# Local and summary attention with a spatially gated MLP: transposes, mixing and plan changed

## Chip, cores and metric

The kernel runs on one core of one Trainium2 chip, as one launch. The metric is the device time of that core in microseconds. The core has five engines that work side by side, each through its own instructions in a fixed order: TensorE (PE, matmuls and transposes; PEld is its loading of weights), VectorE (DVE), ScalarE (ACT), GpSimd (POOL) and SyncE (SP), from whose queue nearly all DMAs are issued.

## The reference

Attention, for batch 4, 8 heads, sequence 768, head size 64, in float32: every query looks at the keys nearer than 16 positions, and beside them at 24 summaries, one for each block of 32 positions. A summary key is the maximum over its block, a summary value the mean.

```
k_sum = k.reshape(B, H, nb, 32, D).max(axis=3)
v_sum = v.reshape(B, H, nb, 32, D).mean(axis=3)
scores_l = where(|i - j| < 16, q @ k.T / 8, -1e9)
scores_s = q @ k_sum.T / 8 + log(32)
a = softmax(concat([scores_l, scores_s], -1))       # eps 1e-9 in the denominator
x = (a @ concat([v, v_sum])), heads side by side     # 4 x 768 x 512
h = relu(x @ w_in);  u, v = halves of h              # 512 each
v_n = (v - mean) / sqrt(var + 1e-6)
out = (u * (w_spatial @ v_n + b_spatial)) @ w_out    # 4 x 768 x 512
```

`w_in` (512 x 1024) and `w_out` (512 x 512) arrive as float64, all else as float32.

## The kernel before

**Attention** goes in 24 groups: 4 batches, 3 chunks of 256 positions (`c`), 2 sets of 4 heads (`g`). For one group, `scores` (L411) makes 16 products of 64 queries with 120 keys (64 + 2 x 16 near ones and 24 summaries), in half-array tiles, into PSUM tile `s`. Each of the two "heads" `a` of a group (in fact two heads stacked on the 128 partitions) then has its softmax in four pieces on DVE (L425) and ScalarE (L429), the inverse of the sums (L434, L435) and a scaling (L437). `trans` (L450) turns the probabilities over on TensorE, 8 transposes of 64 rows for each head, into one PSUM tile `t` of two banks of 512 float32 that both heads share; two copies bring it to SBUF (`pt`), one by ScalarE and one by DVE, after both heads. `mix` (L468) multiplies by the values `ve` (16 products of 64 columns), and the result is split into two `fp32r` parts, high and low, on ScalarE (`xh`, L481) and DVE (`xl`, L482).

Scores, transposes and mixing of a group use half of the array's rows, columns or both at a time, while the dense tiles use the full array; so do the transposes of value means, `vmp` (L381), with all 128 partitions, 128 moving columns and 88 weight columns.

**The dense part** of a batch has four kinds of tiles: `proj_v` (6 tiles `pv`, 12 matmuls of 512 columns each), `proj_u` (`pu`: 4 tiles of 12 x 512 and 4 of 12 x 256), `spatial` (`sp`: 4 of 18 x 512 and 4 of 18 x 256) and `proj_out` (`po`, 6 of 12 x 512). `mm3` (L501) makes each product of high and low parts as three matmuls, hence steps of three that an attention piece can come between. The four share three one-bank PSUM tiles `m`.

**Weights** come by DMA and are split into high and low parts on ScalarE, DVE and POOL: `w_in` for `v` first (`wwi` matmuls help), then for `u`, `w_spatial` (`ws`) and `w_out` (`wo`).

**The order** of all engines is written out ahead by a planner, `Plan`. Each step is added with the engines that can do it and a duration for each, a priority, and what it reads and writes. `order` then always takes the step that can start first, the lower priority among equals, and places it on the engine that ends it first. A step's result counts as there after `LAG` of its engine, for TensorE's use a further `SLACK` of 500 ns later. A DMA's arrival is modelled by `WIRE` and a rate, and at most eight are under way. The order that comes out is fixed: an engine whose next instruction waits runs nothing else. Priorities are times in microseconds: attention group `i` has `at(i)`, and the dense tiles follow a counter `dense`. Where the plan leaves TensorE idle before a point early in the kernel, throw-away matmuls (`warm`, L670) fill the time.

```python
    SLOTS = dict(s=1, t=1, x=1, m=3, k=4, vt=1, p=4, pt=3, ...
    LAG = dict(PE=250, ACT=150, DVE=150, POOL=150, SP=0)
                t = min(from_(op, at, e) for e in op.engs)
                if best is None or (t, op.pri, op.n) < best:
                u.ready = max(u.ready, op.end if e == "PE" and "PE" in u.engs else done + (SLACK if "PE" in u.engs else 0))
```

Of the kernel before, what the change touches and what calls it, by code (L numbers as in the profile page):

```python
# [59 lines left out]
class Op:  # L60
    __slots__ = ("engs", "fn", "pri", "after", "users", "need", "ready", "bufs", "start", "end", "eng", "n", "port", "xfer")


class Plan:


    SLOTS = dict(s=1, t=1, x=1, m=3, k=4, vt=1, p=4, pt=3, x01h=2, x01l=2, x2h=2, x2l=2, g=NG, e=3, u=1, vnh=1, vnl=1,
# [3 lines left out]
    LAG = dict(PE=250, ACT=150, DVE=150, POOL=150, SP=0)  # L71

    def __init__(self):
        self.ops, self.wrote, self.read, self.turn, self.late = [], {}, {}, {}, set()

    def add(self, engs, fn, pri, w=(), r=(), port=False, xfer=0):
# [4 lines left out]
        op.fn, op.pri, op.users, op.n = fn, pri, [], len(self.ops)  # L81
        op.port, op.xfer = port, xfer
# [13 lines left out]
        for x in (*w, *r):  # L96
            if isinstance(x, Buf) and not x.ops and x.tag in self.TURNS and x.args[4][:2] not in self.OUT_OF_TURN :
# [7 lines left out]
    def order(self):  # L105
# [4 lines left out]
        waiting = {}  # L110
# [7 lines left out]
        made, landed, wire, port = [], [], 0, 0  # L118
# [9 lines left out]
        while pool:  # L128
# [20 lines left out]
            op.end = op.start + op.engs[e]  # L149
            op.eng = e  # L150
# [9 lines left out]
            done = op.end + self.LAG[e]  # L160
# [19 lines left out]
def tile_local_summary_attention_gmlp(ctx: ExitStack, tc: tile.TileContext, qT, kext, vpad, vnat, vT, w_in, w_sp, b_rep, w_out, maskc, out):  # L180
# [39 lines left out]
    def early(name):  # L220
        return EARLY.get(name, 0.0)

    def dma(out_, in_, kb, pri, w=(), r=(), issue=420, rate=RATE):
        add(("SP", issue), lambda e: nc.sync.dma_start(out=out_() if callable(out_) else out_, in_=in_() if callable(in_) else in_), pri, w, r, xfer=kb * 1024 / rate)
# [12 lines left out]
    def split32(src, hi, lo, name, pri, key):  # L237

        n = src.shape[-1]
        st = Buf(moe, [P, 2 * TH], F32, "g", name)  # L240
        dma(lambda: st.t[:, :n], src, n * 0.5, pri + early("d" + key[1:]), w=[st])
        pri += early(key)
        add(("ACT", act_ns(n)), lambda e: nc.scalar.copy(out=hi, in_=st.t[:, :n]), pri, w=[key + "h"], r=[st])
        add(two_ns(n), lambda e: eng(e).tensor_sub(out=lo, in0=st.t[:, :n], in1=hi), pri, w=[key + "l"], r=[st, key + "h"], port=True)

    def split64(st, so, f, fo, src, hi, lo, pri, key, on_pe=False):

        if src.dtype != I64:
            n = src.shape[-1]
            dma(lambda: st.t[:, so:so + n], src, n * 0.5, pri, w=[(st, so), st])  # L250
            add(("ACT", act_ns(n)), lambda e: nc.scalar.copy(out=hi, in_=st.t[:, so:so + n]), pri, w=[key + "h"], r=[(st, so), st])
            add(two_ns(n), lambda e: eng(e).tensor_sub(out=lo, in0=st.t[:, so:so + n], in1=hi), pri, w=[key + "l"], r=[(st, so), st, key + "h"], port=True)
            return
# [6 lines left out]
        dma(raw, src.bitcast(I32), n, pri + early("d" + key[1:]), w=[kr], r=[st])  # L260
        pri += early(key)

        add(("ACT", act_ns(n)), lambda e: nc.scalar.activation(out=fv(), in_=words(1).bitcast(F32), func=AF.Copy, scale=2.0 ** -112), pri, w=[kf], r=[kr, st, f])
        add(("DVE", n * 0.72 + 60), lambda e: nc.vector.tensor_scalar(out=fi(), in0=fi(), scalar1=3, scalar2=None, op0=ALU.logical_shift_left), pri, w=[kf], r=[st, f], port=True)
        add(("DVE", n * 1.05 + 65), lambda e: nc.vector.scalar_tensor_tensor(
            out=fi(), in0=words(1), scalar=-2 ** 31, in1=fi(), op0=ALU.bitwise_and, op1=ALU.bitwise_or), pri, w=[kf], r=[kr, st, f], port=True)

        add(("DVE", n * 0.72 + 60), lambda e: nc.vector.tensor_scalar(out=words(1), in0=fi(), scalar1=-2 ** 23, scalar2=None, op0=ALU.bitwise_and), pri, w=[kr + (1,)], r=[kr, kf, st, f], port=True)
        add(("ACT", act_ns(n)), lambda e: nc.scalar.copy(out=hi, in_=fv()), pri, w=[key + "h"], r=[kf, f])
        add(("DVE", n * 1.05 + 65), lambda e: nc.vector.scalar_tensor_tensor(  # L270
            out=words(0).bitcast(F32), in0=words(0).bitcast(U32), scalar=2.0 ** -52, in1=words(1).bitcast(F32),
            op0=ALU.mult, op1=ALU.mult), pri, w=[kr + (0,)], r=[kr, kr + (1,), st, f], port=True)
        if on_pe:
# [7 lines left out]
            add(("PE", 2000), mm, pri, w=[ps], r=[key + "h", kf, kr + (0,), st, f, negid[0]])  # L281
            add(dict(ACT=act_ns(n), DVE=dve_ns(n)), lambda e: copy(e, lo, ps.t[:, :n]), pri, w=[key + "l"], r=[ps])
# [6 lines left out]
    def win_load(half, pri):  # L289
# [5 lines left out]
        for c in range(NC):  # L295
            if half == 0 and c > 1:
                for o in range(0, DF, TH):
                    st = Buf(moe, [P, 2 * TH], F32, "g", f"wi{half}_{c}_{o}")
                    f = Buf(moe, [P, DF], F32, "e", f"wf{half}_{c}_{o}")
                    first(st, f, pri)  # L300
# [3 lines left out]
            if c % 2 == 0:  # L304
                tag = ("u", None, "vnl", "vnh")[2 * half + c // 2]
                stages[c // 2] = Buf(big, [P, 3 * 1024], F32, tag, f"wi{half}_{c}")
                first(stages[c // 2], None, pri)
# [24 lines left out]
    def key_load(b, pr, pri):  # L332
        kt = k_sb[b, pr] = Buf(att, [P, KC], F32, "k", f"k{b}_{pr}")
        dma(lambda: kt.t, kext[b, pr], 544, pri, w=[kt])

    def key_prep(b, pr, pri):
        kt = k_sb[b, pr]
        gm = Buf(small, [P, 52], F32, "gm", f"gm{b}_{pr}")

        def emit(e):  # L340
# [32 lines left out]
    def vmean(b, pr, pri, buf):  # L373
        vt = Buf(att, [P, S], F32, "vt", f"vt{b}_{pr}")
        dma(lambda: vt.t, vT[b, pr], 384, pri + VT_OFF, w=[vt])
        vs = vs_in[:, pr * SEG:(pr + 1) * SEG]
        add(("DVE", 880), lambda e: nc.vector.tensor_reduce(
# [3 lines left out]
        add(("PE", 110), lambda e: nc.tensor.transpose(out=ps.t[:SEG, :P], in_=vs, identity=ident), pri, w=[ps, f"ves{buf}_{pr % 2}"], r=[f"vs{pr}"])  # L381
# [5 lines left out]
    def q_load(b, c, g, buf, pri):  # L387
        dma(qd[buf], qT[b, c, g], 256, pri, w=[f"q{buf}"])

    def v_load(b, c, g, buf, pri):  # L390
        s0 = c * CH
        fs = slice(2 * g * P, 2 * (g + 1) * P)
        dma(ve[buf][:QB], vpad[b, s0:s0 + CH, fs].rearrange("(i p) f -> p i f", p=QB), 256, pri, w=[f"vea{buf}"], issue=620, rate=RATE_64)
        dma(ve[buf][SEG:],
            vpad[b, s0 + QB:s0 + QB + CH, fs].rearrange("(i p) f -> p i f", p=QB)[:2 * WIN], 128, pri, w=[f"veb{buf}"], issue=620, rate=RATE_32)
# [3 lines left out]
    def scores(b, c, pg, buf, pri):  # L399


        ps = Buf(ps_s, [P, 2, 512], F32, "s", f"s{b}_{c}_{pg}")
        kts = [k_sb[b, 2 * pg + r] for r in range(2)]
# [10 lines left out]
        add(("PE", 1000), mm, pri, w=[ps], r=[*kts, f"q{buf}"])  # L414
# [3 lines left out]
    def softmax(u, ps, pri):  # L418
        b, c, pg, a = u
        pt = p_sb[u] = Buf(att, [P, BPU, KW], F32, "p", f"p{b}_{c}_{pg}_{a}")  # L420
        st = Buf(sums, None, None, "st", f"st{b}_{c}_{pg}_{a}")
        for i in range(BPU):
            g = c * BPU + i
            mi = 0 if g == 0 else (2 if g == NSEG - 1 else 1)
            add(("DVE", 205), lambda e, i=i, mi=mi: nc.vector.tensor_tensor_reduce(  # L425
# [5 lines left out]
                accum_out=st.t[:, 1, i:i + 1]), pri, w=[(pt, i)], r=[pt, st])  # L431

        def inverse(e):
            nc.vector.tensor_scalar_add(out=st.t[:, 1, :], in0=st.t[:, 1, :], scalar1=EPS_SM)  # L434
            nc.vector.reciprocal(out=st.t[:, 0, :BPU], in_=st.t[:, 1, :BPU])  # L435
        add(("DVE", 380), inverse, pri, w=[(pt, "i")], r=[(pt, i) for i in range(BPU)] + [st, pt])
        add(dict(DVE=590, POOL=1080), lambda e: eng(e).tensor_tensor(  # L437
# [3 lines left out]
    def trans(b, c, pg, pri):  # L441


        ps = Buf(ps_t, [P, 2, 512], F32, "t", f"t{b}_{c}_{pg}")
        for a in range(2):
            def mm(e, a=a, pt=p_sb[b, c, pg, a]):
                for i in range(BPU):
                    for r in range(2):
                        hs = slice(r * QB, (r + 1) * QB)
                        nc.tensor.transpose(out=ps.t[:KW, r, a * CH + i * QB:a * CH + (i + 1) * QB], in_=pt.t[hs, i, :], identity=ident[hs, hs])  # L450
            pt = p_sb.pop((b, c, pg, a))
            add(("PE", 300), mm, pri, w=[(ps, a)], r=[(pt, "n"), pt, ps])
        for r in range(2):
            tt = pt_sb[b, c, 2 * pg + r] = Buf(att, [KW, 2 * CH], F32, "pt", f"pt{b}_{c}_{pg}_{r}")
            add(dict(ACT=510, DVE=600), lambda e, tt=tt, r=r: copy(e, tt.t, ps.t[:KW, r]), pri, w=[tt], r=[(ps, 0), (ps, 1), ps])
# [3 lines left out]
    def mix(b, c, g, buf, pri):  # L459
        ps = Buf(ps_x, [P, 2, CH], F32, "x", f"x{b}_{c}_{g}")  # L460
        tts = [pt_sb.pop((b, c, 2 * g + r)) for r in range(2)]

        def mm(e):
            for r in range(2):
                for n in range(BPU):
                    for a in range(2):
# [4 lines left out]
                            rhs=tts[r].t[:, a * CH + n * QB:a * CH + (n + 1) * QB],  # L471
                            start=True, stop=True)
        add(("PE", 1050), mm, pri, w=[ps], r=[*tts, f"vea{buf}", f"veb{buf}", f"ves{buf}_0", f"ves{buf}_1"])
# [7 lines left out]
        add(("ACT", 520), lambda e: nc.scalar.copy(out=h.t[:, :, fs], in_=ps.t), pri, w=[kh], r=[ps, h])  # L481
        add(("DVE", 610), lambda e: nc.vector.tensor_sub(out=l.t[:, :, fs], in0=ps.t, in1=h.t[:, :, fs]), pri, w=[kl], r=[ps, kh, h, l])  # L482
# [35 lines left out]
    def proj_v(b, t, pri):  # L518
        s = batch_state(b)
        c, o = divmod(t * P, CH)  # L520
        ps = Buf(ps_m, [P, 512], F32, "m", f"pv{b}_{t}")
# [237 lines left out]
```

## Time and profile before

| | |
|---|---|
| median of 3 runs | 427.93 us (427.31 to 428.41) |
| span of the profiled execution | 426.5 us, 9422 instructions |
| between the two | 1.4 us |
| PE busy | 413.7 us (97%), 3604 matmul records |
| DVE / ACT / POOL busy | 269.2 (63%) / 214.1 (50%) / 52.8 (12%) |
| HBM | 40.16 MB read, 6.29 MB written |

The page gives no time of the profiled execution other than its span, from the first instruction to the last; the difference to the median is what lies around it. Records of matmuls overlap, since matmuls are pipelined: the record of a 512-column matmul in the dense part is some 390 ns long, while the next starts some 227 ns later. So the distances between starts, and the chain of waits, which cuts pieces where the next begins, are the way to price TensorE's work. The granted clock (PEclk) is a share of full speed, which is 2.4 GHz; a half is 1.2 GHz. In the chain of waits, `x6` behind a piece counts its instructions. A scores or mixing matmul in float32 is recorded as two instructions, so `s x32` is 16 products.

### The profile page before, as it was taken

How to read it: one execution, taken by the hardware profiler on the slowest of the kernel's cores; microseconds unless marked ns; L12 is line 12 of the kernel's file. 1: busy time of each engine (PE TensorE's matmuls, PEld its weight loads, DVE VectorE, ACT ScalarE, POOL GpSimd, SP SyncE). 2: the span in 40 equal slices, each digit the busy share in tenths (PEclk: the TensorE clock that was granted, in tenths of full speed). 3: DMA queues.
4: the chain of work that ended last, by engine and by line, in shares of the span. 5: the costliest groups of instructions: out<-in, count | busy, mean ns of one | idle time of the engine just before them, and what ended most of it. 6: DMA issues, size and time to landing. Idle time of an engine off the chain costs nothing.

```text
span 426.5 us, 9422 instructions
## 1 busy us (share of the span) xinstructions
PE 413.7 (97%) x3604; PEld 333.0 (78%) x3604; DVE 269.2 (63%) x927; ACT 214.1 (50%) x655; POOL 52.8 (12%) x72
## 2 busy tenths in 40 slices
PE   8999977999999999999999999999999999999995
PEld 8557755788887878788787877788787978898884
DVE  4778999889993988384661967366582546135402
ACT  5389965686263656463442657364273344231221
POOL 1046843110000012010000001110000002010000
PEclk9999996999999999999999999999999999999998
DMA  7998999151025942322023652102103010000021
GB/s 291 382 319 234 269 274 270 34 162 38 0 63 164 330 132 68 99 77 60 4 63 112 209 165 62 38 26 62 38 26 112 26 51 1 0 2 0 2 98 49
DMA packets 25741, 47.06 MB, mean 110 GB/s; under 512 B 2528, under 2 KB 12640, under 8 KB 25568
## 3 DMA queue, kind: packets, MB, share of 16 engines
q1 hardware_dynamic: 25616, 46.33, 35.6%
q8 instruction: 28, 0.46, 0.4%
q10 hardware_dynamic: 80, 0.13, 0.1%
q14 instruction: 17, 0.14, 0.1%
HBM read 40.16 MB, written 6.29 MB: 109 GB/s over the span
## 4 chain that ended last, share of the span: by engine, by line
PE 90%; DMA 7%; ACT 1%; DVE 1%; POOL 0%; issue 0%; DVEq 0%; SPq 0%; POOLq 0%
PE sp L501 24%; PE pu L501 16%; PE po L501 16%; PE pv L501 14%; PE x L468 5%; PE s L411 5%; DMA ve<-in_vpad_dram 4%; PE t L450 3%; PE warm L670 3%; DMA ws<-in_w_sp_dram 2%; PE vsum L364 1%; PE wwi L280 1%; PE wwi L278 1%; PE vmp L381 0%; DVE p L425 0%; ACT ve L383 0%
## 5 line engine op out<-in xcount | busy, mean ns | idle before, releaser
L429 ACT ACTIVATE p<-p,sums 128x120 f32<-128x120 f32 x192 | 73.5, 385 | 4.6 <-DVE sums L425 4.5
L501 PE MATMUL sp<-wsp_h,vnh 128*128 128x512 f32 (+1 forms) x192 | 66.6, 347 | 0.0
L501 PE MATMUL sp<-wsp_l,vnh 128*128 128x512 f32 (+1 forms) x192 | 64.7, 337 | 0.0
L501 PE MATMUL sp<-wsp_h,vnl 128*128 128x512 f32 (+1 forms) x192 | 64.5, 336 | 0.0
L425 DVE CUSTOM_DVE_ANT_0 p<-s,mask 128x120 f32<-128x120 f32 x192 | 42.1, 277 | 17.9 <-PE s L411 17.7
L501 PE MATMUL po<-wo_h,gt 128*128 128x512 f32 x128 | 48.1, 404 | 0.0
L501 PE MATMUL pu<-xh,win_h 128*128 128x512 f32 (+1 forms) x128 | 44.7, 349 | 0.0
L573 ACT CAST gt<-g 128x512 fp32r<-128x512 f32 (+1 forms) x32 | 16.4, 512 | 55.2 <-DVE g L566 52.0
L501 PE MATMUL pu<-xl,win_h 128*128 128x512 f32 (+1 forms) x128 | 43.2, 337 | 0.0
L501 PE MATMUL pu<-xh,win_l 128*128 128x512 f32 (+1 forms) x128 | 43.0, 336 | 0.0
L501 PE MATMUL pv<-win_h,xh 128*128 128x512 f32 x96 | 41.0, 427 | 1.6 <-ACT ve L383 1.6
L501 PEld LDWEIGHTS sp<-wsp_h,vnh 128*128 128x128 f32 x192 | 36.3, 189 | 5.5 <-issue 1.1
L501 PEld LDWEIGHTS sp<-wsp_h,vnl 128*128 128x128 f32 x192 | 36.4, 190 | 4.0
L501 PEld LDWEIGHTS sp<-wsp_l,vnh 128*128 128x128 f32 x192 | 36.4, 190 | 3.5
L501 PE MATMUL pv<-win_l,xh 128*128 128x512 f32 x96 | 38.3, 399 | 0.0
L565 DVE TENSOR_TENSOR g<-sp,brep 128x512 f32<-128x512 f32 (+1 forms) x32 | 17.6, 552 | 32.7 <-PE sp L501 32.7
L501 PE MATMUL pv<-win_h,xl 128*128 128x512 f32 x96 | 38.0, 396 | 0.0
L501 PE MATMUL po<-wo_l,gt 128*128 128x512 f32 x96 | 37.6, 392 | 0.0
L429 ACT ACTIVATION_READ_ACCUMULATOR p<-p,sums 128x1 f32 x192 | 36.3, 189 | 0.0
L535 POOL TENSOR_TENSOR mv<-mv,mhalf 128x1 f32<-128x1 f32 x24 | 16.6, 694 | 135.4 <-DVE mv L533 127.8
L482 DVE TENSOR_TENSOR xl<-x,xh 128x512 fp32r<-128x512 f32 x24 | 16.5, 688 | 22.4 <-ACT xh L481 22.3
L595 ACT COPY ob<-po 128x512 f32<-128x512 f32 x23 | 13.5, 587 | 33.8 <-PE po L501 28.2
(106 smaller groups left out, 786.7 us busy)
## 6 DMA issues: line engine op xcount, KB each, us to landing
k<-in_kext_dram SPq DMA_DIRECT2D x16, 544.0 KB, 7.5
qd<-in_qT_dram SPq DMA_DIRECT2D x24, 256.0 KB, 4.5
ve<-in_vpad_dram SPq DMA_DIRECT2D x24, 256.0 KB, 3.8
out_dram<-ob SPq DMA_DIRECT2D x23, 256.0 KB, 2.0
vt<-in_vT_dram SPq DMA_DIRECT2D x12, 384.0 KB, 3.6
wi<-in_w_in_dram SPq DMA_DIRECT2D x6, 512.0 KB, 5.5
ve<-in_vpad_dram SPq DMA_DIRECT2D x24, 128.0 KB, 3.6
wo<-in_w_out_dram SPq DMA_DIRECT2D x8, 256.0 KB, 6.6
```

What stands on the lines that cost most here:

```text
L411: nc.tensor.matmul(out=ps.t[r * QB:(r + 1) * QB, a, i * KW:(i + 1) * KW], lhsT=qt[hs, r, i], rhs=kts[r].t[hs, g * SEG:g * SEG + KW], start ...
L425: add(("DVE", 205), lambda e, i=i, mi=mi: nc.vector.tensor_tensor_reduce(out=pt.t[:, i, :], in0=ps.t[:, a, i * KW:(i + 1) * KW], in1=mask[ ...
L429: add(("ACT", 380), lambda e, i=i: nc.scalar.activation(out=pt.t[:, i, :], in_=pt.t[:, i, :], func=AF.Exp, scale=-1.0, bias=st.t[:, 0, i:i ...
L450: nc.tensor.transpose(out=ps.t[:KW, r, a * CH + i * QB:a * CH + (i + 1) * QB], in_=pt.t[hs, i, :], identity=ident[hs, hs])
L468: nc.tensor.matmul(out=ps.t[a * D:(a + 1) * D, r, n * QB:(n + 1) * QB], lhsT=ve[buf][:, n, o:o + D], rhs=tts[r].t[:, a * CH + n * QB:a * C ...
L482: add(("DVE", 610), lambda e: nc.vector.tensor_sub(out=l.t[:, :, fs], in0=ps.t, in1=h.t[:, :, fs]), pri, w=[kl], r=[ps, kh, h, l])
L501: nc.tensor.matmul(out=ps.t[:, :n], lhsT=x, rhs=y, start=(j == i == 0), stop=(j == last and i == 2))
L535: add(("POOL", 500), lambda e: nc.gpsimd.tensor_tensor(out=mv.t[:, 1:2], in0=mv.t[:, 1:2], in1=mhalf, op=ALU.pow), pri, w=[mv])
L565: add(("DVE", dve_ns(n)), lambda e: nc.vector.tensor_add(out=g.t[:, :n], in0=ps.t[:, :n], in1=brep[:, ts]), pri, w=[g], r=[ps, "brep"])
L573: add(("ACT", act_ns(n)), lambda e: nc.scalar.copy(out=gh[1](), in_=g.t[:, :n]), pri, w=[kh], r=[g, gt])
L595: add(("ACT", 520), lambda e: nc.scalar.copy(out=ob.t, in_=ps.t), pri, w=[ob], r=[ps])
L670: nc.tensor.matmul(out=warm.t[:, :KW], lhsT=ident, rhs=ident[:, :KW], start=True, stop=True)
```

## The change

- **Transposes.** A head's 8 transposes of 64 rows become 4 of 128 rows, into a one-bank tile `t` of its own. There is one slot for such a tile, so the second head's transposes follow the first head's copy. A copy now belongs to a head, and mixing reads the new layout.
- **PSUM.** The bank that comes free makes a fourth projection tile `m`.
- **Mixing and scores.** From group 8 on, scores of a group and mixing of the group before are one step of the plan: the 32 instructions of the mixing, directly behind them the 32 of the scores. That makes 16 such pairs. The first group of the next batch is added ahead of the dense tiles of a batch.
- **Planner.** Durations and lags are other figures; a change of tile mode on TensorE is charged (187 ns to or from full-array mode, 143 between the two others); several DVE steps are split into their single instructions; `SLACK` falls from 500 to 2, and `RATE` rises from 330 to 365. A two-engine step that is planned to start before 46 us goes to POOL unless DVE would end it 56 us sooner.
- **Offsets.** A table `SHIFT` of 151 entries adds to the priority of single steps; `d...` are DMAs (`dws`, `dwo`: spatial and output weights).

The diff, cut to its core:

```diff
-    SLOTS = dict(s=1, t=1, x=1, m=3, ...
-    LAG = dict(PE=250, ACT=150, DVE=150, POOL=150, SP=0)
+    SLOTS = dict(s=1, t=1, x=1, m=4, ...
+    LAG = dict(PE=240, ACT=140, DVE=120, POOL=90, SP=0)
+    TURN_ROUND, TURN_OVER = 187, 143
...
+        op.fn, op.pri, op.users, op.n = fn, pri + SHIFT.get(op.tag, 0.0), [], len(self.ops)
...
+            if e == "PE":
+                if op.mode[0] != mode:
+                    op.end += self.TURN_ROUND if "d" in (op.mode[0], mode) else self.TURN_OVER
+                mode = op.mode[-1]
...
-        add(("PE", 1000), mm, pri, w=[ps], r=[*kts, f"q{buf}"])
+        if with_ is None:
+            add(("PE", S_NS), mm, pri, w=[ps], r=[*kts, f"q{buf}"], mode="s")
+        else:
+            mix_, pri_, wm, rm, after = with_
+
+            def both(e):
+                mix_(e)
+                mm(e)
+            plan.tag = f"xs{b}_{c}_{pg}"
+            add(("PE", X_NS + S_NS + Plan.TURN_OVER), both, pri_, w=[*wm, ps], r=[*rm, *kts, f"q{buf}"], mode="xs")
+            after()
...
-        ps = Buf(ps_t, [P, 2, 512], F32, "t", f"t{b}_{c}_{pg}")
         for a in range(2):
-            def mm(e, a=a, pt=p_sb[b, c, pg, a]):
+            ps = Buf(ps_t, [P, 512], F32, "t", f"t{b}_{c}_{pg}_{a}")
+            pt = p_sb.pop((b, c, pg, a))
...
+            def mm(e, a=a, pt=pt, ps=ps):
                 for i in range(BPU):
-                    for r in range(2):
-                        hs = slice(r * QB, (r + 1) * QB)
-                        nc.tensor.transpose(out=ps.t[:KW, r, a * CH + i * QB:a * CH + (i + 1) * QB], in_=pt.t[hs, i, :], identity=ident[hs, hs])
...
-            add(("PE", 300), mm, pri, w=[(ps, a)], r=[(pt, "n"), pt, ps])
...
+                    nc.tensor.transpose(out=ps.t[:KW, i * P:(i + 1) * P], in_=pt.t[:, i, :], identity=ident)
+            add(("PE", 340), mm, pri, w=[ps], r=[(pt, "n"), pt])
+            tt = pt_sb[b, c, pg, a] = Buf(att, [KW, 2 * CH], F32, "pt", f"pt{b}_{c}_{pg}_{a}")
+            add(dict(ACT=psa_ns(512), DVE=dve_ns(512)), lambda e, tt=tt, ps=ps: copy(e, tt.t, ps.t[:KW]), pri, w=[tt], r=[ps])
...
-                            rhs=tts[r].t[:, a * CH + n * QB:a * CH + (n + 1) * QB],
+                            rhs=tts[a].t[:, n * P + r * QB:n * P + (r + 1) * QB],
...
-        mix(b, c, g, buf, pri + early(f"x{i}"))
+        m = mix(b, c, g, buf, pri)
+        if i + 1 >= MERGE_FROM and i + 1 < NGRP:
+            waiting.append((m[0], at(i + 1) - LEAD, *m[2:]))
+        else:
+            plan.tag = f"xs{b}_{c}_{g}x"
+            add(("PE", X_NS), m[0], m[1], w=m[2], r=m[3], mode="x")
+            m[4]()
...
-        for i in range(2 * NCH * b, 2 * NCH * (b + 1)):
+        for i in range(2 * NCH * b + (b > 0), min(2 * NCH * (b + 1) + 1, NGRP)):
...
+U_BIG, MERGE_FROM, LEAD = 2, 8, 0.0
+SHIFT = dict(
...
+    dv0_0_0=3, dv0_0_1=106, dv0_1_0=257, dv1_1_0=36, dv2_0_0=263, dvn=38, dvt1_0=469, dvt1_1=13, dwi0_2_256=108,
...
+    dwo1_256=467, dwo2_0=599, dwo2_256=628, dwo3_0=418, dwo3_256=45, dws0_0=575, dws0_512=491, dws1_0=8, dws1_512=518,
...
-SLACK = 500.0
-FAVOUR, BUSY = 1760.0, 55780.0
-WIRE, RATE, RATE_64, RATE_32 = 2200, 330.0, 210.0, 195.0
+SLACK = 2.0
+FAVOUR, BUSY = 56326.0, 46130.0
+WIRE, RATE, RATE_64, RATE_32 = 2300, 365.0, 188.0, 208.0
+S_NS, X_NS = 816, 916
...
+def psa_ns(n):
+    return 58 + n * 0.828
```

## Rows read from the trace of the kernel before

**Rows 1.** Windows: per stretch busy us (x instructions) of PE, PEld, DVE, ACT, POOL; PEclk, DMA, GB/s

```profile
2.50:39.40 36.90, 36.20 (x366) 26.38 (x365) 26.63 (x105) 24.80 (x78) 9.12 (x11) 1.00 0.95 331
39.40:61.60 22.20, 22.15 (x298) 15.96 (x297) 20.22 (x85) 20.35 (x73) 15.08 (x16) 1.00 1.07 266
61.60:69.07 7.47, 1.95 (x35) 1.35 (x35) 7.40 (x16) 4.29 (x9) 2.17 (x2) 0.78 1.05 264
69.07:73.00 3.93, 3.93 (x10) 3.12 (x11) 3.79 (x12) 1.59 (x3) 0.57 (x2) 0.54 0.94 261
73.00:421.90 348.90, 348.80 (x2898) 285.46 (x2896) 210.57 (x713) 160.95 (x491) 24.34 (x31) 1.00 0.24 73
```

**Rows 2.** Windows of L670, the throw-away matmuls: PE, PEld busy, PEclk, DMA, GB/s

```profile
2.50:39.40 36.90, 15.13 (x100) 14.20 (x99) 1.00 0.95 331
```

**Rows 3.** Waits of PE, 61 to 70 us: total us, times, longest us

```profile
PE vmp L381 <- ACT vf L528: 3.1, 1, 3.1
PE pv L501 <- ACT ve L383: 1.6, 1, 1.6
```

**Rows 4.** Chain of waits, 39 to 70 us: start us, us, what

```profile
55.87 10.06 DMA ws<-in_w_sp_dram
...
65.95 0.41 ACT wsp_h L243
```

**Rows 5.** Chain of waits, whole span: four tiles of dense matmuls in a row

```profile
401.11 10.91 PE po L501 x48
```

**Rows 6.** Chain of waits: both heads' transposes and a mixing among projections

```profile
127.74 0.38 PE t L450 x8
128.12 1.60 PE po L501 x6
129.72 0.38 PE t L450 x8
130.10 2.29 PE po L501 x9
132.40 1.08 PE x L468 x32
133.48 4.31 PE po L501 x18
```

**Rows 7.** Chain of waits: scores ahead of a projection

```profile
338.29 0.98 PE s L411 x32
339.27 2.26 PE pv L501 x9
```

**Rows 8.** Chain of waits: scores, two value-mean transposes, projection

```profile
165.60 0.98 PE s L411 x32
166.58 0.35 PE vmp L381 x2
166.93 6.18 PE pu L501 x27
```

**Rows 9.** Chain of waits: a head beside scores, and two heads together

```profile
143.28 0.98 PE s L411 x32
144.26 0.38 PE t L450 x8
...
249.62 0.62 PE t L450 x16
```

**Rows 10.** Groups by line, PE: the value-mean transposes; busy us, mean ns

```profile
L381 PE MATMUL vmp<-ident,vs_in 128*88 128x128 f32 x12 | 3.0, 306 | 4.0 <-ACT vf L528 3.1 <-ACT ve L383 0.8
```

**Rows 11.** Tile t, 100 to 350 us: ns min/median/max, first and last start

```profile
L230 ACT COPY pt<-t x18: 586/587/593, 117.6 to 346.0; 120x512 f32<-120x512 f32 x18
```

**Rows 12.** Timeline of PE: scores directly behind a mixing

```profile
49.19 1.15 PE L468 MATMUL x<-pt,ve 120*64 120x64 f32 x32
50.27 1.05 PE L411 MATMUL s<-k,qd 64*64 64x120 f32 x32
```

**Rows 13.** Timeline of SP's queue: start us, us

```profile
24.89 2.80 SPq L224 DMA_DIRECT2D ws<-in_w_sp_dram  x6
```

More of the change, by code (lines that the diff above doesn't have):

```diff
@@ L60 @@
 class Op:
-    __slots__ = ("engs", "fn", "pri", "after", "users", "need", "ready", "bufs", "start", "end", "eng", "n", "port", "xfer")
+    __slots__ = ("engs", "fn", "pri", "after", "users", "need", "ready", "bufs", "start", "end", "eng", "n", "port", "xfer", "mode", "tag", "lat")
 class Plan:
-    SLOTS = dict(s=1, t=1, x=1, m=3, k=4, vt=1, p=4, pt=3, x01h=2, x01l=2, x2h=2, x2l=2, g=NG, e=3, u=1, vnh=1, vnl=1,
+    SLOTS = dict(s=1, t=1, x=1, m=4, k=4, vt=1, p=4, pt=3, x01h=2, x01l=2, x2h=2, x2l=2, g=NG, e=3, u=1, vnh=1, vnl=1,
                  gm=2, st=8, bs=4, mv=4)
@@ L109, in order @@
         left = {}
-        waiting = {}
         for op in self.ops:
@@ L117, in order @@
         pool = [op for op in self.ops if not op.need]
-        made, landed, wire, port = [], [], 0, 0
+        made, landed, wire, port, mode = [], [], 0, 0, "d"
         def from_(op, at, e):
@@ L218, in tile_local_summary_attention_gmlp, with dma @@
     ve = [const.tile([KW, BPU, 2 * P], F32, name=f"ve{g}") for g in range(2)]
[L220 to L224, printed above, removed]
+    def dma(out_, in_, kb, pri, w=(), r=(), issue=400, rate=RATE, tag=None):
+        add(("SP", issue), lambda e: nc.sync.dma_start(out=out_() if callable(out_) else out_, in_=in_() if callable(in_) else in_), pri, w, r, xfer=kb * 1024 / rate, tag=f"d{tag}")
     def eng(e):
@@ L295, in win_load @@
         for c in range(NC):
-            if half == 0 and c > 1:
+            if half == 0 and c >= U_BIG:
                 for o in range(0, DF, TH):
@@ L594, in proj_out @@
         else:
-            add(("ACT", 520), lambda e: nc.scalar.copy(out=ob.t, in_=ps.t), pri, w=[ob], r=[ps])
-            dma(out[b, rows, :], lambda: ob.t, 256, pri, r=[ob])
+            add(("ACT", psa_ns(512)), lambda e: nc.scalar.copy(out=ob.t, in_=ps.t), pri, w=[ob], r=[ps])
+            dma(out[b, rows, :], lambda: ob.t, 256, pri, r=[ob], tag=f"o{b}_{t}")
     def group(i):
@@ L619, in attention @@
             for r in range(2):
[L620 to L621 removed]
+                key_load(b, 2 * g + r, pri - 6)
+        q_load(b, c, g, buf, pri - 6)
         if i == 0:
[L623 to L624 removed]
+            dma(mask, maskc, 180, pri - 5, w=["mask"], rate=RATE_64, tag="mask")
+        v_load(b, c, g, buf, pri - 4)
         if c == 0:
             for r in range(2):
[L627 to L628 removed]
+                key_prep(b, 2 * g + r, pri + KP_OFF)
+        scores(b, c, g, buf, pri, waiting.pop() if waiting else None)
         if b == c == g == 0:
```

165 lines of the change are left out of this document (88 added, 77 removed).

## Prediction

> **What bounds the kernel now.** I read the windows first, with borders put where TensorE's timeline changes character. From 73.0 to 421.9 us TensorE is busy 348.80 of 348.90 us at full granted clock, while DMA is at a quarter and no other engine is near full: for 82% of the span the time is what TensorE has to do, and nothing else [rows 1]. Ahead of that lie three stretches of another kind. Up to 39.4 us the DMA engines are at 0.95 and 331 GB/s, and TensorE fills its time with 100 throw-away matmuls, 15.13 us by their records [rows 1, 2]. From 39.4 to 61.6 us it is dense. From 61.6 to 69.07 us it works 1.95 of 7.47 us, and the ten matmuls after it run at a granted clock of 0.54, which is mostly the lower level of 1.2 GHz, until 73 us [rows 1].
>
> The waits name the stall: TensorE stood 3.1 us at a value-mean transpose (`vmp`) for ScalarE's evacuation `vf`, and 1.6 us at the next projection for ScalarE's copy `ve` [rows 3]. The chain of waits says why: a piece of the spatial weights, issued at 55.87, landed 10.06 us later, ScalarE's cast of it stood in ScalarE's order ahead of `ve`, and TensorE, whose order is fixed too, stood behind `ve` [rows 4]. So the order was planned for a DMA that came too late.
>
> Next, what TensorE's pieces cost inside the dense stretch. The chain of waits gives starts, so a piece is priced by the time to a later start less the plain matmuls between at their pace, 10.91 us for 48, 0.2273 each [rows 5]. Two heads' transposes, from 127.74 to 132.40 with 15 projection matmuls between: 4.66 - 3.41 = 1.25, so 0.625 a head, although the piece itself shows as 0.38: the rest is the return to full-array matmuls, the first six of which take 1.60 for 1.36 [rows 6]. Mixing: 5.39 (1.08 + 4.31) less 18 x 0.2273 = 1.30, of which 0.22 is such a return [rows 6]. Scores: 0.98 + 2.26 - 9 x 0.2273 = 1.19, of which 0.21 [rows 7]. Scores with two `vmp` transposes behind them: 0.98 + 0.35 + 6.18 - 27 x 0.2273 = 1.37 [rows 8].
>
> **The change, part by part.** All sums are of the profiled span, 426.5 us; the median of the timed runs, 427.93, lies 1.4 above it, and I carry that 1.4.
>
> *Transposes.* A head had 8 transposes of 64 rows in half-array tiles; it gets 4 of all 128 rows in full-array mode, the mode of the matmuls around it, so the return goes. The nearest row of an operation like the new ones is `vmp`, a full-height float32 transpose with 128 moving columns: the pair cost 1.37 - 1.19 = 0.18, 0.09 each [rows 7, 8]. A head after: 4 x 0.09 = 0.36, a gain of 0.265. After 39.4 us, where TensorE is the bound, the timeline has 43 heads: 11.4 us. Off that go 8 places where a head stood directly beside scores or mixing and shared the return (one of them [rows 9]; 8 x 0.2) and two where both heads ran as 16 in 0.62 and cost 0.82 instead of 1.25 (2 x 0.43) [rows 9]: 11.4 - 2.5 = **8.9 us gained**. Bounds: at the `vmp` record's own 306 ns, unhidden, a loss of 37 (below); at no cost at all, 15.5 more than taken. I stay at 0.09, measured in the stream.
>
> That record's 306 ns [rows 10] and the pair's 0.09 are two readings of one thing. The Trainium skill (TensorE: Matmul & The Clock Gate, Part 4: PE-mode transpose) gives about 275 ns for a 128x128 bf16 transpose inside a kernel and says that transposes don't engage the fast clock. By it 8 x 0.275 = 2.2 us a group would be an estimate of the new cost, against 1.25 now, so a loss. By that rule the pair should have cost 0.55; the trace has 0.18, and the clock of the dense stretch, with 36 heads of transposes in it, stayed at 1.00. Its result stands among the rivals.
>
> *One bank a head.* Copies of head 0 now start before head 1's transposes, but these must wait for that copy, 0.587 us on ScalarE [rows 11], plus about 0.16 for the matmul's tail (record 0.39 against pace 0.23). Behind that wait stands all of TensorE. Between heads the trace has 1.98 us (127.74, 129.72 [rows 6]), filled with projection matmuls that stay there, so I take 0. If the cover goes (a copy late by a full interval) it is at most 24 x 0.75 = 18; below zero it can give nothing, since TensorE has no idle time there.
>
> *Mixing directly ahead of the next scores*, for groups 7 to 22, 16 times. In the trace scores start 1.08 after a mixing in front of them, as long as the mixing itself [rows 12]: no return between. So one return of 0.21 goes each time: **3.4 us gained**. Bounds 0 to 16 x 0.22 = 3.5. The pair now waits for both parts' inputs, with every projection queued behind. Scores come some 4 us sooner after a mixing than before (mixing ends at 133.48, scores at 137.79), so their q and k transfers must too; DMA at 0.24 there leaves room [rows 1].
>
> *A fourth projection buffer, smaller DVE and ScalarE steps, first group of the next batch planned earlier.* The same instructions; TensorE waits for none of them after 73 us, so 0. They are cover for the parts above.
>
> *Measured times and offsets.* (a) Nearly all transfers of the spatial and output weights get offsets of 200 to 650, that is, behind any other ready transfer of SP's queue. This is the transfer at the head of the stall. The stall is 7.47 - 1.95 = 5.5, and the slow stretch 3.93 less 10 x 0.2273 = 1.7 [rows 1]: **7.2 us gained** if nothing else is late there. Late next: the same weights at the first spatial matmuls, some 30 us on. All of them, 4.5 MB by the tile sizes, take 17 us at 264 GB/s [rows 1], so there is room. (b) Before 39.4 us six of these pieces hold SP's queue for 2.80 us from 24.89 on [rows 13], and their 1.2 MB (three of 256 and three of 128 KB) are 3.6 us of DMA at 331 GB/s. Moved back, that helps q and v of the first groups by 0 to 3.6, or hurts by as much if the table's other entries delay v, q and the values' sums too far; I take the middle of the gain, about **2.0 gained**. (c) The reserve ahead of TensorE falls from 500 ns (SLACK) to 2. After 73 us the trace has no wait; 54 stops (36 heads, 18 mixings) can now have one, from 0 to 54 x 0.5 = 27. The new model's 482 + 140 ns for a 512-column copy out stands against a record of 587 [rows 11], a difference of 0.04, so I take 0.04 a stop: **2.0 lost**.
>
> Sum: 426.5 - 8.9 - 3.4 - 7.2 - 2.0 + 2.0 = 407.0; with the 1.4, **408.4 us**.
>
> **The rivals.**
> - *The early stall comes back* elsewhere before 110 us (a weight's cast ahead of an evacuation on ScalarE, again behind a DMA), with its slow clock. For: DVE is busy 7.40 of 7.47 us of that stretch, and full-rate DMA is modelled faster than before. Against: the transfers in question go last. 408.4 + 7.2 = 415.6.
> - *The start shortens fully and nothing is late*: (b) 3.6, (c) 0: 408.4 - 1.6 - 2.0 = 404.8. For: 15 us of throw-away matmuls [rows 2]. Against: DMA at 0.95 with loads that are needed anyway.
> - *Slower: no reserve.* The place is TensorE's stops after 73 us: each head and each mixing is set to the very moment at which the model has its input ready; a late softmax or copy holds all projections behind it. Price: the lost 500 ns at 54 stops, 27: 408.4 + 25 = 433.4. It decides from (427.9 - 406.4) / 54 = 0.40 a stop. Against: durations in the new model are those of the trace, and a wait at one stop lets the next inputs catch up.
> - *Slower: transposes don't overlap*, each 0.306 instead of 0.09: 0.216 x 4 x 43 = 37, so 445.6. For it: the record's length [rows 10]; against it: the pair. The Trainium skill's page on TensorE, as above, would have it so.
>
> **How the numbers follow.** Forecast 0.58, the stall back 0.20, the short start 0.15, no reserve 0.05, transposes unhidden 0.02. 401 to 418 holds the forecast with its open terms, the case of the stall and most of the short start, about 0.87. Less than 0.3% (1.3 us) can't be told from no change. Faster: the first three, 0.93; within 0.3%: a part of "no reserve", 0.01; slower 0.06.
>
> **What would show it.** Transposes: 192 instead of 384, a head in a dense stretch at 0.36 with no long first matmul behind it. Merging: 16 pieces of mixing and scores 1.08 apart, one return behind. Stall: no wait over 1 us and no granted clock under 1 between 40 and 420 us. Reserve: waits of TensorE at L450 and L468 in the table of waits, summing to about 2. Start: first projection at about 37 us. The prediction is wrong if heads cost 0.6 or more, if TensorE's waits after 73 us exceed 5 us, or if the first projection comes later than 44.

## The result, and the profile after

The changed kernel takes 414.75 us (median of 4 runs, 413.80 to 418.43), the kernel before 427.99 beside it (427.31 to 428.41): a ratio of 0.9712, 95% interval 0.967 to 0.9753. The profiled execution took 414.29 us, its span is 412.5, with 1.8 between the two. The forecast was 408.4, with a span of 407.0: the gain came, 13.2 us of the 19.5 expected.

The windows of after, cut where its character changes, answer to [rows 1]; the columns are the same.

```profile
2.50:38.59 36.09, 34.79 (x337) 25.46 (x337) 27.41 (x116) 25.21 (x81) 9.22 (x11) 1.00 1.01 343
38.59:63.00 24.41, 23.03 (x251) 18.33 (x249) 23.19 (x88) 19.39 (x70) 8.89 (x8) 1.00 1.05 272
63.00:73.00 10.00, 10.00 (x77) 8.40 (x76) 9.94 (x26) 6.82 (x14) 3.41 (x5) 1.00 0.87 257
73.00:407.80 334.80, 334.80 (x2743) 284.58 (x2741) 201.39 (x699) 164.86 (x498) 19.89 (x31) 1.00 0.24 75
```

The hole of 5.5 us and the stretch at the lower clock are gone: the granted clock is 1.00 throughout, and TensorE has no idle time from 63 us to its last matmul, which ends at 407.8. In their place 1.4 us of small waits lie between 38.59 and 63. The throw-away matmuls, 100 in 15.13 us in [rows 2], are 90 in 12.79 us, and the first projection comes at 38.59, not 39.46. The waits of TensorE over the whole span (total us, times, longest) answer to [rows 3]:

```profile
PE warm L619 <- POOL ident masks.py:199: 1.8, 1, 1.8
PE s L405 <- DVE wf L261: 0.9, 1, 0.9
PE s L405 <- ACT k L344: 0.8, 1, 0.8
PE t L455 <- DVE p L441: 0.4, 1, 0.4
PE x L471 <- DVE pt L232: 0.3, 1, 0.3
PE x L471 <- DVE xl L489: 0.2, 1, 0.2
```

None of them lies after 73 us. The chain of waits prices the new transposes (start us, us, what), against [rows 6]:

```profile
265.32 0.44 PE t L455 x4
265.75 1.40 PE pv L508 x6
267.15 0.44 PE t L455 x4
267.59 1.39 PE pv L508 x6
268.98 2.88 PE pu L508 x24
271.86 0.22 PE vmp L374 x2
272.08 2.05 PE pu L508 x9
```

Two heads with 12 projection matmuls take 268.98 - 265.32 = 3.66; less 12 x 0.2273 that is 0.93, or 0.466 a head. Behind a head the next six matmuls now take 1.39 to 1.40, near their 1.36: the return is gone, as forecast. But the four transposes themselves cost 0.44, where 0.36 was forecast for the head with all that belongs to it. The pair of `vmp` that follows costs 0.22; the nine matmuls of 512 columns behind it go at their pace, 2.05. The merged pair, in the same view, answers to [rows 7] and [rows 12]:

```profile
137.73 1.08 PE x L471 x32
138.82 0.98 PE s L405 x32
139.80 1.60 PE po L508 x6
```

Scores begin 1.09 after the mixing, and one return follows, 1.60 - 1.36 = 0.24.

### The profile page after: what moved, and what is told of

Read it like the earlier page. It is cut to its first block, busy times and chain, and to the rows that moved or that the text cites. A ratio compares the mean times of both kernels' runs of the same rounds, so it can differ in the third digit from the quotient of the medians.

```text
span 412.5 us, 9001 instructions
## 1 busy us (share of the span) xinstructions
PE 403.4 (98%) x3402; PEld 337.5 (82%) x3402; DVE 262.6 (64%) x925; ACT 218.5 (53%) x663; POOL 42.9 (10%) x66
## 4 chain that ended last, share of the span: by engine, by line
PE 91%; DVE 5%; DMA 1%; ACT 1%; issue 1%; POOL 0%; SPq 0%; DVEq 0%; ACTq 0%; POOLq 0%
PE sp L508 24%; PE po L508 16%; PE pu L508 16%; PE pv L508 13%; PE s L405 5%; PE x L471 5%; PE t L455 4%; PE warm L690 2%; DMA qd<-in_qT_dram 1%; PE vsum L356 1%; DVE p L430 1%; PE wwi L276 1%; PE wwi L274 1%; ACT p L434 1%; DVE wi L266 1%
## 5 line engine op out<-in xcount | busy, mean ns | idle before, releaser
L434 ACT ACTIVATE p<-p,sums 128x120 f32<-128x120 f32 x192 | 73.3, 385 | 12.3 <-DVE sums L430 12.2
L430 DVE CUSTOM_DVE_ANT_0 p<-s,mask 128x120 f32<-128x120 f32 x192 | 42.2, 278 | 28.1 <-PE s L405 27.9
L508 PE MATMUL pv<-win_h,xh 128*128 128x512 f32 x96 | 38.9, 405 | 0.0
L232 ACT COPY pt<-t 120x512 f32<-120x512 f32 x35 | 20.6, 587 | 34.1 <-PE t L455 33.9
L471 PEld LDWEIGHTS x<-pt,ve 120*64 120x64 f32 x768 | 24.6, 138 | 7.6 <-issue 5.3
L542 POOL TENSOR_TENSOR mv<-mv,mhalf 128x1 f32<-128x1 f32 x24 | 13.6, 579 | 161.2 <-DVE mv L541 88.4
```

Of the source, the lines that this page charges most:

```text
L232: (nc.scalar.copy if e == "ACT" else nc.vector.tensor_copy)(out=out_, in_=in_)
L430: add(("DVE", 203), lambda e, i=i, mi=mi: nc.vector.tensor_tensor_reduce(out=pt.t[:, i, :], in0=ps.t[:, a, i * KW:(i + 1) * KW], in1=mask[ ...
L434: add(("ACT", 380), lambda e, i=i: nc.scalar.activation(out=pt.t[:, i, :], in_=pt.t[:, i, :], func=AF.Exp, scale=-1.0, bias=st.t[:, 0, i:i ...
L471: nc.tensor.matmul(out=ps.t[a * D:(a + 1) * D, r, n * QB:(n + 1) * QB], lhsT=ve[buf][:, n, o:o + D], rhs=tts[a].t[:, n * P + r * QB:n * P ...
L508: nc.tensor.matmul(out=ps.t[:, :n], lhsT=x, rhs=y, start=(j == i == 0), stop=(j == last and i == 2))
L542: add(("POOL", 560), lambda e: nc.gpsimd.tensor_tensor(out=mv.t[:, 1:2], in0=mv.t[:, 1:2], in1=mhalf, op=ALU.pow), pri, w=[mv])
```

## The experiments

Twelve kernels ran beside before and after; e1, which only prices blocks of transposes, is not in the table. A time is a median; "waits" are TensorE's by the table of waits, the 1.8 of the warm-up at the start left out, and "from 60" is the part of them from 60 us on; "softmax" is the number of DVE's masking steps of `p` (L430 in after, L425 in the kernel before) that start between 60 and 100 us, 8 to a group. Nearly all of these are the second batch's (in e6 5 of the 22 are the first's), so they count how much of its attention is worked on while weights are still being split.

| kernel | us | ratio to before, 95% | waits | from 60 | softmax |
|---|---|---|---|---|---|
| before | 428.0 | | 6.1 | 5.5 | 23 |
| after | 414.75 | 0.967 to 0.9753 | 2.6 | 0.4 | 0 |
| e2, pair split | 420.67 | 0.9815 to 0.985 | 5.3 | 1.3 | 0 |
| e3, three buffers | 429.59 | 1.0027 to 1.0059 | 12.2 | 8.3 | 0 |
| e4, e3 and half-row transposes | 434.09 | 1.0093 to 1.0169 | 12.2 | 8.2 | 0 |
| e5, empty table | 420.76 | 0.9781 to 0.9857 | 8.3 | 4.4 | 16 |
| e6, only 20 weight offsets | 419.88 | 0.9766 to 0.9832 | 8.3 | 3.6 | 22 |
| e7, before with those 20 | 429.16 | 0.9991 to 1.0038 | 10.5 | 5.8 | 19 |
| e9, three buffers, empty table | 421.48 | 0.9792 to 0.9865 | 8.9 | 4.8 | 16 |
| e10, only two offsets | 414.85 | 0.967 to 0.9736 | 4.0 | 0 | 0 |
| e11, all but those two | 418.84 | 0.9768 to 0.9824 | 5.2 | 2.7 | 16 |
| e12, before with those two | 428.45 | 0.9994 to 1.0025 | 5.5 | 4.9 | 23 |
| e13, three parts in one step, plan set anew | 410.25 | 0.9532 to 0.9599 | 3.8 | 0 | 0 |

### What a transpose costs (e1)

Blocks of transposes are appended behind the last matmul, six plain matmuls between blocks.

```diff
...
+    for _ in range(32):
+        nc.tensor.transpose(out=bt[:KW, 0, :P], in_=src, identity=ident)
+    pad()
...
+    for i in range(64):
+        hs = slice(i % 2 * QB, (i % 2 + 1) * QB)
+        nc.tensor.transpose(out=bt[:KW, i % 2, :QB], in_=src[hs], identity=ident[hs, hs])
...
```

> The changed kernel with blocks of transposes and projection matmuls added behind its last matmul, for their prices alone; its time is longer by them and says nothing. Theory A (the step of a full-height transpose is set by the load of its weight columns): 120 weight columns 0.11 us each, 88 columns 0.08, 64 columns 0.06, 128 columns 0.115; with 64 rows in alternating row halves 0.025 each, in one row half alone about 0.1; four full ones with three matmuls 0.68 + 0.45 = 1.13, eight half ones with three matmuls 0.68 + 0.60 = 1.28. Rival B (it is set by the 128 moving columns, at half the rate of the fp32r matmuls): 0.11 for 120, 88, 64 and 128 weight columns alike, and 0.055 for 64 moving columns.

The timeline of TensorE around the first block (start us, us from the first start to the last end):

```profile
411.19 3.65 PE L722 MATMUL bench<-ident,mask 128*120 128x128 f32 x32
414.60 1.64 PE L718 MATMUL bench<-win_h 128*128 128x512 f32 x6
```

The chain of waits through all blocks: 120, 88 (left out), 64 and 128 weight columns, then half rows in two banks, half rows in one, and a round of each mixture.

```profile
411.35 3.49 PE bench L722 x32
...
421.12 3.49 PE bench L728 x32
...
426.00 3.49 PE bench L731 x32
...
430.89 2.00 PE bench L735 x64
...
434.48 3.84 PE bench L739 x64
...
447.89 0.44 PE bench L743 x4
448.33 0.70 PE bench L714 x3
...
455.49 0.38 PE bench L749 x8
455.87 0.89 PE bench L714 x3
```

A full transpose costs 0.107 (414.60 - 411.19 = 3.41 for 32) whatever the width of its weights, so the theory that the weight columns set it fell. The rival's price for 128 moving columns, 0.11, is what was found; that the moving columns set it stays argued, since no block varies them alone (the half rows have half the rows as well). Half rows alternating between two row halves and two banks go at 2.00 / 64 = 0.031, in one half and one bank at 3.84 / 64 = 0.060, where the rival had 0.055 for both; but they have the return behind them (0.89 for three matmuls, not 0.70). A head among projections is 0.44 + 0.70 - 0.68 = 0.46 in the full form and 0.38 + 0.89 - 0.68 = 0.59 in the half form; the kernels' own streams gave 0.466 and 0.625.

The Trainium skill (TensorE: Matmul & The Clock Gate, Part 4: PE-mode transpose) gives about 275 ns for a 128x128 bf16 transpose inside a kernel. The record of these float32 ones agrees (192 in after, mean 274 ns), the stream does not: they start 0.107 apart. The same section of the Trainium skill says that the fast clock doesn't engage for transposes. The granted clock in the block of 32, which follows dense matmuls, was 1.00; whether transposes alone would raise or hold it no run shows. The Trainium skill (TensorE: Matmul & The Clock Gate, LDWEIGHTS (loading the stationary operand)) has the weight load grow with the columns of the weights. The records of the loads in e1 do grow (medians of 111, 123, 138 and 140 ns for 64, 88, 120 and 128 columns); the pitch of the transposes doesn't.

### What merging is worth (e2)

The same order, but the scores are issued one TensorE step after the mixing.

```diff
             def both(e):
                 mix_(e)
-                mm(e)
+                later.append((mm, e))
...
```

> The changed kernel in its own order, but each of the 16 merged scores comes one TensorE step after its mixing, three projection matmuls in most places. Theory (one return to full-array matmuls costs 0.21 and merging saves it): 16 x 0.21 = 3.4 us slower than the changed kernel, mixing and scores each with a long first matmul behind. Rival (the return is hidden by the loads, merging gave nothing and the whole gain is the plan's): same time as the changed kernel within 1 us.

```profile
212.43 1.08 PE x L472 x32
213.51 0.90 PE po L509 x3
214.41 1.02 PE s L406 x32
```

In its chain of waits the three projection matmuls between take 0.90 instead of 0.68: a second return of 0.22. From the first spatial to the last matmul e2 takes 328.60, after 323.41; of these 5.19 some 1.4 are new waits of transposes for the softmax that the later scores delay, and 3.8 remain, 0.24 for each of the 16 pairs, which is the return. That is the theory's term; another 1.5 us lie before the first spatial matmul, where TensorE waits 1.2 for a transfer of q and 1.5 ahead of a mixing, against 1.3 in after, and don't belong to it.

### The fourth buffer and the form of the transposes (e3, e4, e9)

e3 takes one buffer away (`m=4` to `m=3`), e9 does so with an empty table, e4 is e3 with half-row transposes into two banks:

```diff
-            ps = Buf(ps_t, [P, 512], F32, "t", ...)
+            ps = Buf(ps_t, [P, 2, 512], F32, "t", ...)
...
-                    nc.tensor.transpose(out=ps.t[:KW, i * P:(i + 1) * P], in_=pt.t[:, i, :], identity=ident)
+                    for r in range(2):
+                        hs = slice(r * QB, (r + 1) * QB)
+                        nc.tensor.transpose(out=ps.t[:KW, r, i * QB:(i + 1) * QB], in_=pt.t[hs, i, :], identity=ident[hs, hs])
...
```

> The changed kernel with three projection buffers in place of four, planned anew. Theory (the fourth buffer is cover only; TensorE does not wait for evacuations): within 1.5 us of the changed kernel's 414.8. Rival (the table of offsets fits one plan only, any change of it brings waits): 418 to 424, with TensorE's waits before 110 us.

> As the run with three projection buffers, with a head's transposes as 8 of 64 rows into two banks, the form of before, in the same order. Theory (a head costs 0.625 in half-array form and 0.47 in full-array form): 43 heads x 0.155 less 2 for neighbours, about 4.5 us slower than with three buffers alone. Rival (the forecast's 0.36 a head): 43 x 0.265 less 2.5, about 9 us slower.

> Three projection buffers and an empty table. Theory (the 13 us that three buffers cost with the table are a table that no longer fits): within 3 us of the run with an empty table and four buffers. Rival (the fourth buffer itself is worth 13 us, since evacuations then no longer hold TensorE): 10 us or more slower than that run.

e3 is 15 us above after, above even its rival's range, with waits of TensorE in every stretch but that from 100 to 130 us. That is not the buffer: without the table three buffers take 421.48 and four 420.76, a difference of 0.7, with intervals that overlap. It is the table, made for one order and applied to another. With a table that fits, three buffers were not run beside four. e4 is 4.5 above e3, with the same waits. The forecast's gain of transposes would have made that 9, the price from e1 (0.155 less a head) makes it 4 to 5.

### What the table is worth, and which part of it (e5, e6, e7, e10, e11, e12)

e5 empties `SHIFT`; e6 leaves the 20 offsets of `dws` and `dwo`; e7 gives these 20 to the kernel before. e10 leaves two entries, the preparation of the second batch's first two key pairs (work of DVE and ScalarE):

```diff
...
-    dv0_0_0=3, dv0_0_1=106, ...
+    p1_0=300, p1_1=299)
```

e11 takes out these two alone, and e12 gives them to the kernel before.

> The changed kernel with an empty table of offsets, planned anew. Theory (the table holds the early stall away; the price of attention on TensorE is the same without it): 420 to 428, with TensorE's waits and perhaps a granted clock under 1 before 110 us, and no more than 2 us of waits after. Rival (measured times alone do it, the table adds nothing): 415 +- 1.5.

> The changed kernel with only the 20 offsets of the spatial and output weights' DMAs left in the table. Theory of the forecast (these late transfers are what removes the stall): 415 to 417, no wait over 1 us. Rival (the other 131 entries are needed, an order fits as a whole or not at all): as the run with an empty table, 420 or more.

> The kernel before with these same 20 offsets on the spatial and output weights' DMAs, nothing else changed. Theory of the forecast: the wait for a late weight's cast at 61 to 69 us and the slow clock go, 7.2 us: 420 to 421. Rival (another late arrival takes its place): 426 or more, with a wait over 2 us between 40 and 110 us.

> The changed kernel with all but two entries of the table of offsets taken out: left are p1_0=300 and p1_1=299, which put the preparation of the second batch's keys (DVE and POOL work, and all of that batch's attention that waits for it) behind the first batch's dense tiles. The kernel with an empty table took 420.8 us, with the whole table 414.75. Theory: before 100 us DVE is the bound, and what the table buys is that the second batch's attention is no longer worked on there; these two entries give most of it: 415 to 417 us, TensorE's waits before 130 us at most 4 us (8.4 with the empty table), the scores of group 6 later than 80 us. Rival: the gain is spread over the whole table, as a finished order of all steps: 419.5 to 421.5 us, waits still 7 or more.

> The changed kernel with only those two entries (p1_0, p1_1) taken out of the table; the other 149 stay. Theory (the second batch's attention competes for DVE before 100 us): without them its key preparation comes early again unless other entries of that batch (its value means and mixing, offsets of 200 to 350) hold it back as well; if they do not, the time is near that of the empty table, 419 to 421 us; if they do, 415 to 417 us. Rival (the table is a finished order, from which no entry can be taken): 421 us or more, with waits after 130 us too.

> The kernel before with one thing changed: the preparation of the second batch's keys gets priority offsets of 300 and 299, the two entries that did the work of the whole table in the changed kernel. Nothing of the transposes, the merging, the buffers or the durations is changed. Theory: before's stall at 61 to 69 us is DVE carrying the second batch's attention beside the splitting of weights; with that attention put back, the stall and its slow clock shrink or go, 421 to 425 us, with the granted clock at 1.00 from 60 to 80 us. Rival: the two entries need the changed kernel's durations and its fourth projection buffer to work; in the old order they only move the waits elsewhere: 427 to 430 us.

The table is worth 6.0 us by the medians (4.6 by the two ratios), and two of its 151 entries give all of that; the 20 weight offsets, which the forecast held to be the cure, give 0.9, with intervals that overlap, and nothing in the kernel before. There they did move the transfers (the last piece of `ws` is issued at 71.0 us, not at 55.9), but between 60 and 80 us TensorE still waits 4.2 of the 5.5 us, at a granted clock of 0.83 as before. With the empty table, the larger waits of TensorE and, by the groups of one tile, DVE's masking steps of `p` from 60 to 100 us (ns min/median/max, first and last start):

```profile
PE t L455 <- DVE sums L440: 2.2, 1, 2.2
...
PE s L405 <- ACT k L344: 1.5, 1, 1.5
PE t L455 <- ACT gt L584: 1.1, 1, 1.1
```

```profile
L430 DVE CUSTOM_DVE_ANT_0 p<-s,mask x16: 274/277/282, 77.9 to 90.0; 128x120 f32<-128x120 f32 x16
```

With the two entries, all of TensorE's waits but the warm-up's, and the first masking steps after 60 us:

```profile
PE t L455 <- DVE sums L440: 2.1, 1, 2.1
...
PE t L455 <- POOL p L441: 0.9, 1, 0.9
PE s L405 <- ACT k L344: 0.8, 1, 0.8
PE x L471 <- DVE xl L489: 0.2, 1, 0.2
```

```profile
L430 DVE CUSTOM_DVE_ANT_0 p<-s,mask x8: 278/279/283, 105.0 to 106.4; 128x120 f32<-128x120 f32 x8
```

With the two entries the second batch's first softmax starts at 105 us, not at 77.9, and TensorE works off the first batch's dense tiles meanwhile. The waits halve: those from 60 us on go from 4.4 us to none, the others stay (3.9 and 4.0). The spatial matmuls, which began at 97.7, begin at 84.9. In e11 the rest of the table doesn't hold that batch back: 16 masking steps before 100 us, and a new wait of 2.5 for `pt` between 100 and 130. Without the two entries the whole table loses 4.1 us, with intervals that don't overlap (0.9768 to 0.9824 against 0.967 to 0.9753). Its 418.84 is 2 better than the empty table, with intervals that overlap, and a shade under what was expected for that case.

e12 doesn't test what the two entries do in the old plan, for they left its order as it was. The two key preparations stay at 52.89 and 55.59 us (53.72 and 56.40 before), and so does the stall:

```profile
60.00:80.00 20.00, 15.10 (x105) 11.98 (x94) 19.42 (x59) 11.62 (x30) 3.64 (x4) 0.74 0.49 153
```

(PE busy 15.10 of 20, granted clock 0.74.) The offset decides only among steps that could start at the same moment, and the unchanged order says that in the old plan no other step could.

But e12 is a second look at the old order, in which the transfer at the head of the chain in [rows 4] came in time. Its last piece of `ws` was issued at 52.7 us, not at 55.9, and no cast on ScalarE waits for it, where before ScalarE stood 2.2 us for two such pieces. TensorE's waits in the stall are 3.2 and 1.7, 4.9 after 5.5. So the late transfer made little of the stall. The chain of waits of e12 leads to it through DVE, and the timeline of the kernel before shows the same end:

```profile
55.67 0.86 DVE gm L343
...
57.85 0.84 DVE vs_in L377
...
62.27 0.95 DVE win_l L285 x2
...
63.24 0.61 ACT vf L528
...
63.89 0.44 PE vmp L381
```

```profile
64.06 0.60 ACT L528 ACTIVATE vf<-pv 128x512 f32<-128x512 f32 x1 [1.76 <-DVE win_l L285]
64.71 0.31 PE L381 MATMUL vmp<-ident,vs_in 128*88 128x128 f32 x1 [3.15 <-ACT vf L528]
```

The longest wait of the old stall, 3.1 us, ended at 64.71, before the transfer of [rows 4] landed at 55.87 + 10.06 = 65.93. ScalarE's `vf`, for which TensorE stood, waited for DVE's splitting of `w_in` (`win_l`). In e12's chain DVE works without a break from 55.67 to 63.22; 2.7 of these 7.6 us are key preparation (`gm`, three steps) and value sums (`vs_in`) of the second batch. How much of the old stall would go with them no run shows; what is shown is the price of that batch's attention in the changed kernel.

### A version made from these prices (e13)

From group 8 on one step holds mixing, scores and both heads' transposes, the latter in half rows into two banks, so that all three share one return. The plan's paces and load offsets and a table of 15 entries were set anew for it, which the cut leaves out.

```diff
+        if mx:
+            fns.append(mx[0]); ws += mx[2]; rs += mx[3]; ns += X_NS; modes += "x"
+        if sc:
+            fns.append(sc[0]); ws += sc[1]; rs += sc[2]; ns += S_NS; modes += "s"
+        if tr:
+            ps, pts, mm, evict = tr
+            fns.append(mm); ws.append(ps); rs += [y for pt in pts for y in ((pt, "n"), pt)]; ns += T2_NS; modes += "t"
...
+        add(("PE", ns), lambda e: [f(e) for f in fns], pri, w=ws, r=rs, mode=modes)
```

> A further version: from group 8 on one TensorE step holds the mixing of the group before last, the scores of the next group and, right behind them, both heads' transposes of the last group, in the half-row form into two banks (so three projection buffers); p1_0=300, other offsets found anew for this order (15 entries). Theory, from the prices measured: 16 half-row transposes at 0.031 are 0.50 a group and share the one return behind them, where two heads of full transposes cost 0.93: 16 x 0.43 = 6.9 less than the 414.85 us of the kernel with the two offsets; against that the heads of groups 4 to 7, alone in the half-row form, 8 x 0.13 = 1.0 more, one merging less 0.2, the third buffer 0.7: 410 us, 408 to 412. Rival: the step waits for more inputs at once and projections queue behind it, or mixing a group later holds the dense tiles up: 414 us or more, with waits of TensorE after 130 us.

410.25 us (407.62 to 413.97), the fastest of all: 0.9566 of before, 0.9532 to 0.9599. Its chain of waits and its window after 130 us:

```profile
215.85 1.08 PE x L491 x32
216.93 0.98 PE s L405 x32
217.91 0.62 PE t L463 x16
218.53 4.33 PE po L528 x18
```

```profile
130.00:400.00 270.00, 269.99 (x2324) 230.20 (x2321) 158.16 (x528) 123.14 (x374) 13.41 (x22) 1.00 0.22 72
```

One return, 4.33 - 4.09 = 0.24, behind all three, and no wait. The time is as expected, the term is not: the 16 transposes take 0.62, as in [rows 9], not 0.50, so a group gains 0.31 and not 0.43, 5.0 in all. That would give 414.85 - 5.0 + 1.9 = 411.8; the other 1.5 is either smaller costs or the plan that was set anew, which no run takes apart. That the time fell on the forecast is partly luck.

## Why the prediction came out as it did

By the profiled spans the forecast was 407.0 and the chip gave 412.5, 5.5 more. (The medians differ by 6.35, because the median of the runs lies 2.25 above the span here, not 1.4.) The time lies next to the rival of the stall that comes back, 415.6, but is not that case: no granted clock under 1 and no wait over 1 us shows after 38.59. Windows from the first projection to the last matmul, before and after, with the columns of [rows 1], give the whole gain in parts:

```profile
39.46:421.80 382.34, 376.77 (x3238) 305.83 (x3237) 241.85 (x822) 187.11 (x575) 42.10 (x49) 0.99 0.31 90
38.59:407.82 369.23, 367.85 (x3067) 311.31 (x3065) 234.52 (x809) 191.07 (x581) 32.19 (x43) 1.00 0.31 93
```

The start gives 39.46 - 38.59 = 0.9, idle time falls from 5.6 to 1.4, the slow clock gives 1.7, and the rest, 376.77 - 1.7 - 367.85 = 7.2, is TensorE's own work: 14.0 of 14.0 in all. For that work 8.9 + 3.4 = 12.3 was forecast. Step by step:

- **Transposes: the return goes, right; 0.09 each, wrong.** This is the mis-sized term. A head costs 0.466, so 43 heads gain 43 x 0.159 - 2.5, about 4.3, where 8.9 was forecast: 4.6 of the 5.5. With 3.4 for the merging that makes 7.7, and 7.2 was measured. The price came from a pair of `vmp`, 0.18 as a difference of two sums, 1.37 and 1.19 [rows 7, 8], and such a pair stands beside scores, together with their return. In after one stands among projections and costs 0.22 (at 271.86), 0.11 each. e1 measures 0.107 in a long row, and four of them bring some 0.04 more at their ends. The rival of transposes that don't overlap was rightly given little: 0.27 a record, 0.107 apart.
- **One bank a head: right.** No wait for the copy shows after 73 us; the projections between heads cover it.
- **Merging: right in mechanism and size.** 3.4 forecast; e2 loses 3.8 to the second return.
- **The stall and its clock, 7.2: the size came, the cause was wrong, so that term was luck.** The step "This is the transfer at the head of the stall" failed. The chain of waits [rows 4] ended at a late transfer, but that chain stands only behind the last waits of the stall: the longest had ended before the transfer landed (64.71 against 65.93), and where the transfer came in time (e12) 4.9 of 5.5 us remained. Putting the weights' transfers back (e7) left 4.2 of them and the clock, and in the new kernel (e6) it gave 0.9 of the table's 6.0. What the runs show in its place: DVE full ahead of `vf` in the old order, and in the new kernel the two entries that put the second batch's attention behind the first batch's dense tiles (e10 against e5, e11 against after). The row that pointed there had been read, DVE busy 7.40 of 7.47 us [rows 1]; it stood only as an argument for a rival. Of the kernels above, those with 16 or more masking steps between 60 and 100 us wait 2.7 to 5.8 us from 60 us on, those without 0 to 1.3; exceptions are e3 and e4, whose table doesn't fit (8.3 and 8.2 with none). In the kernel before, e7 and e12 the slow clock comes on top.
- **Small waits in the stall's place: not forecast**, 1.4 us between 38.59 and 63.
- **The start: 2.0 forecast, 0.9 came.** DMA ran at 1.01 and 343 GB/s there, against 0.95 and 331; the loads are needed all the same.
- **No reserve: 2.0 forecast as a loss, 0 came.** TensorE never waits after 73 us. A stop at which the inputs come a little late would show there; none does.

The sum: 4.6 + 1.4 + 1.1 - 2.0 = 5.1 of the 5.5. The miss of the transposes was partly made good by the reserve, which is luck as well.

## What to carry to other kernels

Price a short operation from a long row of itself, or from a place where nothing beside it hides a part; a difference of two sums at a boundary gives the boundary with it. A chain of waits that ends at a late transfer names what came last, not what would have come next: compare the time of its landing with the end of each wait, and ask which engine was full in that stretch, and whose work on it was not yet needed. When a step has to leave the tile mode of its neighbours, put everything that leaves it into one place, so that the return is paid once.

## What was not expected of the hardware

The pitch of a float32 transpose of 128 moving columns, 0.107 us, did not depend on its weight columns (64 to 128), and the granted clock stayed at 1.00 through 32 of them in a row; half-array transposes went at 0.031 each when they alternated between two row halves and two banks, and at 0.060 in one. So the form before was the cheaper one by itself (0.38 a head against 0.44), and lost only by its return of 0.21 to 0.24; in e13, where that return is shared, it wins.
